# One kernel, two total orders: re-sorting the 660 operations of a convolution block and an MLP on one core

## The chip, the cores and the metric

The kernel runs on one core of a Trainium2 chip. The metric is device time in microseconds (us). Five engines with instruction queues of their own take part: TensorE (PE, matrix products and its own weight loads, PEld), VectorE (DVE), ScalarE (ACT), GpSimd (POOL) and SyncE (SP, which here does nothing but issue transfers; its queue is SPq in the profile). Each engine executes its own instructions strictly in their order and waits on semaphores for the others.

## The reference

A sequence of 2048 rows with 640 features goes through two residual blocks.

```python
x  = A_q
h  = x + A(layernorm(x), A_k, A_v, A_shift_k, A_ssm_k, A_ssm_D)
h2 = h + B(layernorm(h), w1, b1, w2)
# A: k_shift = 4-tap causal filter of k with shift_k;  kv = k_shift * v
#    y = (long causal convolution of kv with ssm_k, length 2048) + kv * ssm_D
#    returns layernorm(x) * y
# B: a = mish(layernorm(h) @ w1 + b1)          640 -> 1728
#    returns a @ w2                            1728 -> 640
```

The reference does the long convolution by FFT. The kernel does it with matrix products against tables of cosines and sines, in two factors of 128 and 16 (128 frequencies f, 16 residues), and folds `ssm_D` into the first tap of the filter.

## The kernel before

**How the work is cut.** The 640 features are five chunks of 128 (`dc` 0 to 4), the 2048 rows are 16 tiles of 128 (`t`). PSUM is used as four tiles of 128 x 1024 f32 (banks 0 to 3 below). Nearly every product stage writes one such tile, and a copy by ACT or DVE (the helper at L259 to L263: L261 is ACT, L263 is DVE) takes it back to SBUF as bf16 before the bank can be used again.

**Stages**, with the names that the order uses (a `pe` in a name is the product, an `ev` the copy that empties its bank):

- Loads by SP: `d_n` (the filter `ssm_k`, 5 x 512 KB), `d_k` and `d_v` (4 x 640 KB each), `d_g` (the table G, 8 x 512 KB), `d_x` (the rows x, 4 x 640 KB, into the place of v), `d_t2m` (a table, 1 MB), `d_w1*`, `d_w2*` (weights). ACT issues three small ones: `d_dr` (ssm_D), `d_cst` (tables), `d_sk` (the four taps). POOL issues three tiny ones for the bias b1, inside `small`.
- Filter branch: `dadd` adds D to the first tap (L370), `k1pe`/`k1ev` transpose (L376), `s1kpe`/`s1kev` (L396, L397) make 20 tiles, `s2kpe_f`/`s2kev_f` (L422) make 22 tiles of six frequencies each.
- k branch: `ktpe`/`ktev` transpose k (L341), `ktsh` shifts on POOL (L345). `cfpe` and `coef` spread the taps, and `wsh0` to `wsh3` build four filter matrices from them (L317, a tensor by tensor multiply of 1120 elements, on POOL in the order of before, with `"dve"` as a second choice in `wsh_ops`). `kspe`/`kv` filter and multiply with v (L357, L358, L362).
- Convolution: `s1vpe`/`s1vev` (20 tiles), `s2v0pe`, `s2v1pe`, `s2v2pe` with their copies (8, 4 and 8 tiles), `sw` (ten SP transfers inside SBUF that make a half-swapped copy of the filter's spectrum, L450), `pr` (20 products of spectra on DVE, L461), `i1pe`/`i1ev` (20 tiles, L479), `i2` and `y` (16 tiles, L531, L537).
- First layernorm: `ln1_t` (DVE statistics, three instructions, L510, L511), `ln1p` (three small POOL instructions, L515 to L517), `lnx` (apply; ACT L522 or POOL L524).
- Join: `wb` (L538) and `h` (L540) on DVE, `bn` (statistics, L544, L545), `pow` (two small POOL instructions, L549, L550), `hc` (apply, DVE, L559). The result is transposed: tiles 0 and 1 by PE (`trpe`, `trev`), tiles 2 to 15 by an SP transfer (`tr`, L573).
- MLP in five units of 2, 2, 4, 4, 4 tiles: `m1pe` (L598, L605) with `hb` (Mish on ACT, L620), `m2pe` (L663, L671) with `res` (DVE, L685, L688) and `d_out` (SP, L692).

**What sets the order.** One string, `ORDER`, lists every operation. `_ordered` (L108) turns it into the order in which the operations are emitted; nothing reorders them afterwards, and the waits are put in from the tiles that each operation reads and writes. A token is `name`, then `@bank` for an operation that opens a PSUM tile, or `:a`, `:d`, `:p` to put it on ACT, DVE or POOL where it has a choice.

```python
    for tok in ORDER:
        tok, _, slot = tok.partition("@")
        name, _, eng = tok.partition(":")
        o = by_name[name]
        o.eng = _LETTER[eng] if eng else o.engs[0]
        if o.psum is not None:
            o.psum.slot = int(slot)
```

So three things follow from the string and nothing else: the sequence on each engine and each transfer queue, the engine of each copy, and which PSUM bank each product uses.

Two details count below. `emit_warm` (L282) is one operation on two engines, a DVE memset and an ACT activation that waits for it. `emit_small` (L295) is two POOL memsets and three POOL transfers.

Of the kernel before, what the change touches and what calls it, by code (L numbers as in the profile page):

```python
# [25 lines left out]
ORDER = """
d_dr wz idn d_n0 cz wm@0 small lane d_n1 d_cst d_sk d_n2 warm d_n3 d_n4 d_g0 dsel dcol dadd0 d_k2 k1pe0@1 d_k3 dadd1:p k1pe1@2 d_a12 k1ev0b d_k0 k1ev0
s1kpe0_3@3 k1ev1 s1kpe0_1@0 s1kev0_3 d_k1 s1kpe0_0@1 dadd2 s1kev0_1 s1kpe1_3@2 s1kev0_0:d dadd3:p d_g4 s1kpe0_2@3 k1pe2@0 s1kev0_2 dadd4:p d_g1
s1kev1_3 kz b1pe@1 k1pe4@3 k1ev2 c_b1 cfpe@2 k1pe3@1 k1ev4:a coef d_v0 s1kpe2_0@0 k1ev3 wsh1 s1kpe2_1@2 s1kev2_0 s1kpe4_3@3 d_g7 s1kev2_1:d s1kpe3_1@1
s1kev4_3 s1kpe2_2@0 wsh3 s1kpe1_0@2 s1kev3_1 d_v1 s1kev2_2:d s1kpe4_1@3 d_g2 s1kev1_0 s1kpe3_2@1 s1kev4_1:d s1kpe1_2@0 s1kev3_2 d_g6 ktpe0_0@2 wsh2  # L30
ktpe0_3 ktpe0_2 s1kev1_2 ktpe2_0@3 ktpe2_3 ktpe2_2 d_v2 ktpe2_1 ktpe0_1 ktev2 ktpe1_0@1 ktev0:a ktpe1_1 ktpe1_3 ktpe1_2 s1kpe3_3@0 d_g5 ktev1 ktsh2
s1kpe4_0@3 s1kev3_3 s1kpe1_1@2 ktsh0 s1kev4_0:d d_v3 s1kpe4_2@1 wsh0 s1kev1_1 s1kpe3_0@0 s1kev4_2:d s1kpe2_3@3 s1kev3_0 d_g3 ktpe4_0@2 ktpe4_2 ktpe4_3
s1kev2_3 ktsh1 ktpe3_0@1 ktpe4_1 ktpe3_3 ktev4 ktpe3_1 ktpe3_2 s2kpe_6@0 s2kpe_12@3 ktev3 s2kev_6 kspe0_0@2 s2kev_12 s2kpe_18@0 kv0_0 ktsh3 kspe2_0@1
s2kev_18 ktsh4 s2kpe_42@3 kv2_0 kspe3_0@2 s2kev_42 s2kpe_96@0 kv3_0 s2kpe_24@1 s2kev_96 kspe4_0@3 s2kev_24 kspe1_0@2 kv4_0 s2kpe_108@0 kspe1_1@1 kv1_0
s2kev_108 s2kpe_72@3 kspe0_1@0 d_x1 s2kev_72 kv1_1 d_x0 s2kpe_66@2 s2kpe_102@3 s2kev_66 kv0_1 kspe4_1@1 s2kev_102 s2kpe_120@2 kv4_1 kspe3_1@0
s2kev_120 s2kpe_126@3 kv3_1 s2kpe_78@1 s2kev_126 s2kpe_0@2 s2kev_78 s2kpe_114@3 s2kev_0:d s2kpe_36@0 s2kev_114 s2kpe_54@1 s2kev_36:d s2kpe_84@2
s2kev_54 s2kpe_60@3 s2kev_84 ln1_0 kspe2_1@1 s2kev_60 s2kpe_48@0 kv2_1 ln1p0 s1vpe0_2@2 s2kev_48 s1vpe1_1@3 s1vev0_2:d s1vpe2_1@1 d_x2 s1vev1_1
s1vpe1_0@0 d_x3 s1vev2_1 s1vev1_0:d s1vpe4_3@2 s1vpe3_2@3 s1vev4_3 s1vpe0_0@1 s1vev3_2:d s1vpe2_2@0 s1vev0_0 s2kpe_90@2 s1vpe1_2@3 s1vev2_2 s2kev_90:d
s1vpe0_3@1 s1vev1_2 s1vpe1_3@0 s1vev0_3:d s1vpe0_1@2 s1vev1_3 s1vpe3_0@3 s1vev0_1:d s1vpe4_1@1 s1vev3_0 s2kpe_30@0 s1vev4_1:d s2v0pe_0@2 s2kev_30
s2v0pe_48@3 s2v0ev_0 ln1_1 sw1_0 s1vpe2_0@1 s2v0pe_64@0 sw1_1 s2v0ev_48 lnx0:p s1vev2_0:d s2v0pe_112@2 sw0_0 ln1p1 s2v0ev_64 sw4_0 s2v0pe_32@3  # L40
s2v0ev_112:d s2v0pe_80@1 sw3_1 s2v0ev_32 s1vpe3_1@0 lnx1:p sw0_1 ln1_2 s1vpe4_0@2 s2v0ev_80 sw3_0 s1vpe3_3@3 sw4_1 ln1_3 s1vev3_1 ln1p2 s1vpe2_3@1
sw2_0 s1vev4_0 s1vev3_3:d sw2_1 s1vpe4_2@0 lnx2:p s1vev4_2 s2v0pe_96@2 pr1_64 ln1p3 s2v0pe_16@3 s2v0ev_96 s2v2pe_32@0 s1vev2_3:d lnx3:p s2v0ev_16
s2v2pe_80@2 pr1_96 s2v2ev_32 s2v2pe_112@1 s2v2pe_64@3 s2v2ev_112 pr1_0 s2v2pe_48@0 s2v2ev_64 s2v2pe_0@1 pr0_96 s2v2ev_0 s2v2pe_16@3 pr1_32 s2v2ev_16
s2v1pe_96@1 pr0_64 s2v2ev_48 i1pe1_1@3 s2v2ev_80 s2v2pe_96@0 pr3_0 s2v1ev_96 i1pe1_2@2 pr3_32 i1ev1_1 s2v1pe_64@1 pr0_32 s2v2ev_96 s2v1pe_0@3 i1ev1_2
pr0_0 s2v1pe_32@0 s2v1ev_0 pr3_64 i1pe1_3@2 d_w14 s2v1ev_64 d_w10 i1pe0_2@3 pr3_96 d_w11 s2v1ev_32 d_w12 i1pe0_1@1 pr4_0 d_w13 i1ev1_3 d_t2m i1pe3_3@0
i1ev0_1 pr2_96 i1pe3_1@2 i1ev3_3 pr2_64 i1pe3_0@1 i1ev0_2 i1pe0_3@0 pr2_0 i1ev3_0 i1pe0_0@3 pr2_32 i1ev3_1 i1pe3_2@1 i1ev0_3 pr4_96 i1pe2_0@2 i1ev0_0
pr4_32 i1pe1_0@0 i1ev2_0 i1pe2_2@3 pr4_64 i1ev1_0 i1pe2_1@2 ln1_8 i1ev3_2 i1pe2_3@0 i1ev2_2 ln1_6 ln1p8 i1pe4_3@1 i1ev2_3 ln1_11 i1pe4_0@3 ln1p6
i1ev2_1 i1ev4_3:d i1pe4_2@0 i1ev4_0 lnx6:p i1pe4_1@2 ln1_4 i1ev4_2 ln1p11 i2a1@1 d_w2a i1ev4_1 ln1_14 i2a0@3 d_w2b ln1p4 d_w2c i2b1 ln1_10 i2a2@0 y1
i2b0 i2pe4@2 y0 wb1 i2pe5@1 y4 h1 i2pe8@3 wb0 y5 h0 i2b2 i2a3@2 y8 bn1 i2pe15@1 y2 i2b3 i2pe12@3 bn0 y15 pow1 i2pe13@0 y3 i2pe11@1 pow0 y12 hc1 wb2
trpe1@2 y11 i2pe7@3 hc0 y13 h2 trpe0@1 trev1:a wb3 i2pe6@0 bn2 trev0:a i2pe10@2 y7 m1pe0_3@1 h3 lnx11 pow2 bn3 m1pe0_2@3 y6 hc2 y10 pow3 ln1_7  # L50
m1pe0_1@0 tr2 lnx8 ln1p10 hc3 hb0_3 m1pe0_5@2 wb8 tr3 hb0_2 h8 ln1p7 m1pe0_6@1 ln1_9 hb0_5 m1pe0_4@3 hb0_1 ln1p14 ln1_15 m1pe0_0@2 hb0_6 lnx4 wb6 w2z
m1pe1_0@0 wb11 lnx10 wb4 lnx7:p hb0_4 m1pe1_4@1 ln1_5 ln1p15 hb1_0 m1pe1_5@3 wb7 hb0_0 h4 ln1p5 hb1_4 m1pe1_3@0 bn8 hb1_5 lnx5:p m1pe1_1@2 ln1_13
hb1_3 pow8 m1pe1_2@1 wb5 hb1_1 h6 ln1p9 lnx15 m1pe1_6@3 bn6 hb1_2 h5 i2pe9@0 pow6 hb1_6 bn4 i2pe14@2 lnx9 ln1p13 m2pe0@1 hc6 ln1_12 y9 tr6 y14 lnx13:p
bn5 lnx14 pow4 hc8 h11 pow5 tr8 m2pe1@3 wb14 h7 ln1p12 hc5 hc4 bn7 tr4 lnx12 wb10 pow7 tr5 bn11 m2pe2@0 h10 pow11 bn10 wb13 pow10 hc7 hc11 tr7 wb9
wb15 m2pe3@2 res0 tr11 h9 hc10 d_out0 h14 tr10 h15 res2 bn9 d_out2 m1pe2_3@1 wb12 pow9 bn14 h12 pow14 m1pe2_6@0 hc9 hb2_3 bn15 tr9 hc14 h13 m1pe2_5@1
tr14 hb2_6 bn12 res3 pow12 m1pe2_4@0 res1 d_out3 hb2_5 pow15 hc12 bn13 tr12 m1pe3_0@2 hc15 pow13 hb2_4 tr15 hc13 d_out1 tr13 m1pe2_0@3 hb3_0 m1pe3_2@1
hb2_0 m1pe3_6@0 hb3_2 m1pe2_1@2 hb3_6 m1pe3_5@3 hb2_1 m1pe2_2@1 hb3_5 m1pe3_1@0 hb2_2 m1pe3_3@2 hb3_1 m1pe3_4@3 hb3_3 m2pe4@1 hb3_4 m2pe6@0 m2pe5@2
res4 res6 d_out6 d_out4 m2pe7@3 m1pe4_2@1 res7 res5 d_out7 d_out5 m1pe4_5@0 m1pe4_6@3 hb4_5 hb4_2 m1pe4_4@2 hb4_6 m1pe4_3@0 hb4_4 m1pe4_0@1 hb4_3
m1pe4_1@3 hb4_0 m2pe9@2 hb4_1 m2pe11@0 m2pe8@1 res11 res9 d_out9 d_out11 m2pe10@3 m2pe15a@0 res10 res8 d_out8 m2pe12@2 res15a d_out15a d_out10
m2pe14@3 m2pe13@1 res14 res12 d_out14 d_out12 m2pe15b@0 res13 d_out13 res15b d_out15b  # L60
""".split()
# [672 lines left out]
```

## Time and profile before

| what | value |
|---|---|
| median of 3 runs | 225.41 us (225.4 to 225.89) |
| the profiled execution: span from first to last instruction | 223.5 us |
| what the median has over that span | 1.9 us |
| PE busy, ACT busy, DVE busy, POOL busy | 214.0, 133.0, 133.2, 58.9 us |
| granted TensorE clock | 1.000 throughout |

The page gives the span of the profiled execution and no second time for it. Times inside the profile count from the first instruction. "Busy" for PE includes a matmul's whole flight through the array, so two neighbours overlap and a busy PE can still be held up by its banks. A row of the timeline reads: start, duration, engine, line, operation, output from input with shapes, count; in brackets the idle time before it and what ended it. Adjacent rows of the same kind are merged, so "31.36 ... x34" is 34 copies in 31.36 us.

### The profile page before, as it was taken

The page shows a single profiled execution, that of the slowest core. Times are in us where ns is not written, and L with a number is a line of the kernel's source. Part 1 is how long each engine was busy: PE and PEld are TensorE (multiplying, and loading weights), DVE is VectorE, ACT ScalarE, POOL GpSimd, SP SyncE. Part 2 cuts the span into 40 slices and gives each one's busy share as a digit, 9 for nine tenths or more (in the row PEclk, how much of TensorE's full clock was granted, in tenths as well). Part 3 has the DMA queues.
Part 4 walks back from the last instruction along what each step waited for, and adds up shares of the span by engine and source line. Part 5 has one row for each costly group of instructions (what it writes and reads, how often), then busy time and mean ns, then how long its engine had stood idle before and what let it go on. Part 6 is the DMA issues. An engine that isn't in the chain of part 4 may idle for free.

```text
span 223.5 us, 6119 instructions
## 1 busy us (share of the span) xinstructions
PE 214.0 (96%) x2645; PEld 157.6 (70%) x2650; DVE 133.2 (60%) x232; ACT 133.0 (59%) x182; POOL 58.9 (26%) x120
## 2 busy tenths in 40 slices
...
GB/s 181 390 413 409 412 374 121 143 239 93 375 415 69 258 331 290 124 0 62 1 0 62 84 123 91 118 0 0 3 0 59 59 3 0 0 56 6 76 54 49
DMA packets 19563, 30.98 MB, mean 139 GB/s; under 512 B 10704, under 2 KB 14928, under 8 KB 18768
## 3 DMA queue, kind: packets, MB, share of 16 engines
...
q14 instruction: 6, 0.05, 0.1%
...
## 4 chain that ended last, share of the span: by engine, by line
PE 70%; DVE 13%; DMA 9%; ACT 4%; issue 2%; SPq 1%; POOL 1%; DVEq 0%
PE ps L663 26%; PE ps L598 25%; DVE ks L461 6%; DMA ks<-in_B_w_dram 4%; DMA ks<-ks 3%; PE ps L396 3%; PE ps L422 3%; ACT uv L261 3%; DMA ks<-in_A_ssm_k_dram 3%; PE ps L341 2%; PE ps L376 2%; DVE ks L263 2%; PE ps L357 2%; DVE ra L362 1%; PE ps L397 1%
## 5 line engine op out<-in xcount | busy, mean ns | idle before, releaser
L620 ACT ACTIVATE ks<-ps,b1s 128x512 bf16<-128x512 f32 (+1 forms) x69 | 36.1, 610 | 42.8 <-PE ps L598 30.3
L663 PE MATMUL ps<-ks 128*128 128x320 bf16 (+2 forms) x420 | 58.4, 299 | 0.0
L598 PE MATMUL ps<-G 128*128 128x512 bf16 (+1 forms) x320 | 57.0, 336 | 0.3
L688 DVE TENSOR_TENSOR rb<-ps,rb 128x640 bf16<-128x640 f32 x15 | 11.7, 816 | 68.9 <-PE ps L671 66.5
L663 PEld LDWEIGHTS <-ks 128*128 128x128 bf16 x420 | 40.6, 98 | 17.2 <-issue 1.3
L598 PEld LDWEIGHTS <-G 128*128 128x128 bf16 x325 | 31.3, 98 | 24.4 <-issue 1.1
L261 ACT CAST uv<-ps 128x1024 bf16<-128x1024 f32 x49 | 45.2, 1197 | 0.0
L261 ACT CAST ks<-ps 128x960 bf16<-128x960 f32 (+3 forms) x49 | 39.8, 905 | 8.1 <-PE ps L397 5.0
L461 DVE TENSOR_TENSOR ks<-ks,uv 128x2048 bf16<-128x2048 bf16 x20 | 23.1, 1225 | 0.7 <-DMA ks<-ks 0.7
L422 PEld LDWEIGHTS <-G 128*128 128x128 bf16 x512 | 20.9, 96 | 3.1 <-issue 2.5
L479 PE MATMUL ps<-a_t,ks 128*128 128x128 bf16 x320 | 18.8, 219 | 0.4 <-DVE ks L461 0.3
L479 PEld LDWEIGHTS <-ks 128*128 128x128 bf16 x320 | 18.3, 113 | 0.7 <-DVE ks L461 0.6
L422 PE MATMUL ps<-uv,G 128*128 128x64 bf16 (+1 forms) x384 | 12.8, 186 | 1.8 <-ACT uv L261 1.8
L544 DVE BATCH_NORM_STATS2 st<-rb 128x6 f32<-128x320 bf16 x32 | 14.0, 478 | 0.1
L515 POOL TENSOR_SCALAR ve<-mv 128x1 f32<-128x1 f32 x16 | 4.7, 292 | 34.9 <-DVE mv L511 34.2
L510 DVE BATCH_NORM_STATS2 st<-rb 128x6 f32<-128x320 bf16 x32 | 13.7, 471 | 0.0
L263 DVE CAST uv<-ps 128x1024 bf16<-128x1024 f32 x11 | 12.9, 1204 | 0.1
L362 DVE TENSOR_TENSOR ra<-ps,rb 128x1024 bf16<-128x1024 f32 x10 | 11.9, 1222 | 0.7 <-PE ps L358 0.5
L524 POOL TENSOR_SCALAR ra<-rb,r,nmr 128x640 bf16<-128x640 bf16 x8 | 8.9, 1118 | 10.0 <-PE ps L397 9.3
L422 PE MATMUL ps<-ks,G 128*128 128x160 bf16 x128 | 11.2, 230 | 0.0
L396 PE MATMUL ps<-cst,ra 128*64 128x128 bf16 x160 | 10.6, 219 | 0.7 <-ACT uv L261 0.5
L263 DVE CAST ks<-ps 128x1024 bf16<-128x1024 f32 (+1 forms) x9 | 10.5, 1197 | 0.5 <-PE ps L422 0.3
...
## 6 DMA issues: line engine op xcount, KB each, us to landing
ks<-ks SPq DMA_DIRECT2D x10, 512.0 KB, 6.2
G<-tab_g SPq DMA_DIRECT2D x8, 512.0 KB, 11.4
ks<-in_A_ssm_k_dram SPq DMA_DIRECT2D x5, 512.0 KB, 6.4
...
```

The costliest lines, as they stand in the source:

```text
L261: nc.scalar.copy(o, i)
L263: nc.vector.tensor_copy(o, i)
L362: nc.vector.tensor_tensor(kv_w[:, m, :, 8 * h:8 * h + 8, :], p_.f32().rearrange("p (l t d) -> p d t l", l=4, t=8), raw_v[:, 8 * h:8 * h + ...
L396: nc.tensor.matmul(ps[0:64, dgl, :], lhs, mc, start=True, stop=True)
L422: nc.tensor.matmul(p_.f32()[:, o:o + n], g_v[:, f, :], src[:, :, f, :], start=True, stop=True)
L461: nc.vector.tensor_tensor(o, o, v, ALU.mult)
L479: nc.tensor.matmul(pz[:, dgl, :], KS[:, k, b, :, l], a12[:, k, :], start=k == 0, stop=k == 1)
L510: nc.vector.bn_stats(st1[:, t, hh, :], xt(t)[:, hh * 320:(hh + 1) * 320])
L544: nc.vector.bn_stats(st2[:, t, hh, :], xt(t)[:, hh * 320:(hh + 1) * 320])
L598: nc.tensor.matmul(ph[:, o:o + w], w1[:, dc, fc * P:fc * P + P], lt[:, dc, 0:w], start=dc == 0, stop=dc == NDC - 1)
L620: nc.scalar.activation(hb[:, fc, 0:n], p_.f32()[:, i * 512:i * 512 + n], ACT.Mish, bias=b1s[:, fc:fc + 1], scale=1.0)
L663: nc.tensor.matmul(p_.f32()[:, o:o + n], lhs, w2[:, k, cols:cols + n], start=fc == 0, stop=single and fc == 13)
```

## The change

Only the string `ORDER` differs. The operations, their shapes and their number are the same. The first and the last lines of both strings, and those around the filter matrices and the first inverse products:

```diff
-d_dr wz idn d_n0 cz wm@0 small lane d_n1 d_cst d_sk d_n2 warm d_n3 d_n4 d_g0 dsel dcol dadd0 d_k2 k1pe0@1 d_k3 dadd1:p k1pe1@2 d_a12 k1ev0b d_k0 k1ev0
-s1kpe0_3@3 k1ev1 s1kpe0_1@0 s1kev0_3 d_k1 s1kpe0_0@1 dadd2 s1kev0_1 s1kpe1_3@2 s1kev0_0:d dadd3:p d_g4 s1kpe0_2@3 k1pe2@0 s1kev0_2 dadd4:p d_g1
...
-ktpe0_3 ktpe0_2 s1kev1_2 ktpe2_0@3 ktpe2_3 ktpe2_2 d_v2 ktpe2_1 ktpe0_1 ktev2 ktpe1_0@1 ktev0:a ktpe1_1 ktpe1_3 ktpe1_2 s1kpe3_3@0 d_g5 ktev1 ktsh2
...
-m2pe14@3 m2pe13@1 res14 res12 d_out14 d_out12 m2pe15b@0 res13 d_out13 res15b d_out15b
+idn d_dr wz lane d_n0 cz dsel dcol d_cst dadd0:p d_n1 wm@0 dadd1 k1pe0@1 warm d_n2 d_sk k1ev0b d_n3 d_n4 d_g0 k1pe1@2 s1kpe0_3@3 k1ev0 dadd2 k1ev1:a
+dadd3:p s1kpe0_1@0 d_k2 k1pe2@1 s1kev0_3:d d_k3 k1ev2 s1kev0_1 k1pe3@3 s1kpe0_0@2 kz dadd4:p d_a12 d_k0 s1kpe2_2@0 s1kpe2_1@1 k1ev3 cfpe@3 d_k1 coef
...
+wsh3 ktpe2_1 s1kev3_1 ktpe1_2 ktpe1_1 ktpe0_0@1 ktpe0_3 ktpe0_2 ktpe0_1 ktev1:a d_v1 s1kpe3_0@2 ktev2 s1kpe4_0@3 s1kev3_0 d_v3 s1kpe2_3@0 ktev0 ktsh2
+s1kpe1_2@1 s1kev2_3 ktsh1 s1kev4_0:d s1kpe3_2@2 s1kpe4_2@3 s1kev3_2 ktpe4_0@0 ktpe4_3 s1kev1_2 wsh1:d ktpe4_2 d_g5 ktpe4_1 ktpe3_0@2 ktpe3_2
+s1kev4_2:d ktsh0 ktpe3_1 d_g3 wsh2 s2kpe_126@3 s2kpe_120@1 ktpe3_3 ktev4 s2kev_126 small s2kev_120 s2kpe_102@0 kspe0_0@3 s2kpe_114@1 ktev3 d_g1
...
+d_out7 m2pe13@1 m2pe15b@3 d_out10 res14 d_out11 res12 res13 d_out12 d_out8 d_out14 res15b d_out9 d_out15a d_out13 d_out15b
```

Engine by engine, the differences that are spoken of below:

- **ACT's head.** Before: `d_dr d_cst d_sk warm s1kev0_3`. Now: `d_dr d_cst warm d_sk k1ev1`. On DVE the memset of `warm` now stands behind `dadd1`, which waits for the second filter load.
- **POOL.** Before: `idn small dadd1 dadd3 dadd4 kz wsh1 wsh3 wsh2 ktsh2 ktsh0 wsh0 ktsh1 ktsh3 ktsh4`. Now: `idn dadd0 dadd3 kz dadd4 wsh0 wsh3 ktsh2 ktsh1 ktsh0 wsh2 small ktsh4 ktsh3`.
- **DVE around the k transposes.** Before: `ktev2 ktev1 s1kev4_0 s1kev4_2 ktev4 ktev3`. Now: `ktev2 ktev0 s1kev4_0 wsh1 s1kev4_2 ktev4 ktev3`; `ktev1` is ACT's.
- **Copies per engine**, filter branch up to `s2k`: 16 on ACT in both (14 casts `s1kev`, one `k1ev`, one `ktev`). `s2kev`: ACT 19 and DVE 3 before, 18 and 4 now. `s1vev`, `s2v*ev`, `i1ev` together: ACT 49 and DVE 11 before, 48 and 12 now. `y0`, `y9`, `y14` and `trev0` go from ACT to DVE; the copy of the bias, `c_b1`, goes from 12.65 us behind the spectra of v.
- **SP.** The loads of v and G are interleaved differently behind `d_k1` (now `g6 g7 v2 g4 v0 v1 v3 g5 g3 g1 g2`); only `d_x0` is ahead of the ten `sw`; `d_x2` and `d_t2m` stand behind the sixth `sw`, `d_x1` and `d_x3` among the loads of w1, `d_w2c` behind `tr3`. The transposing transfers of unit 2 go out as `tr6 tr4 tr7 tr5` (before: `tr6 tr8 tr4 tr5 tr7`).
- **DVE statistics of the first layernorm.** Before the first `wb`, ten tiles are done in the order of before (0 1 2 3 8 6 11 4 14 10) and five now (2 1 0 3 4).
- **MLP.** The tiles of the hidden layer come in another order, and some `m1pe` stand between `m2pe`s; all `m1pe0`, `m1pe1`, then `m2pe0` to `m2pe3` still come first, and `m2pe13`, `m2pe15b` last.

59 lines of the change are left out of this document (29 added, 30 removed).

## The prediction

> **What bounds the kernel now.** I read the table of windows first (columns: stretch, then busy us and instruction count of PE, PEld, DVE, ACT, POOL, the granted clock, the DMA share, GB/s).
>
> ```profile
> 27.45:91.20 63.75, 60.07 (x1318) 56.66 (x1316) 61.68 (x75) 61.47 (x68) 16.04 (x30) 1.00 0.68 251
> 99.50:130.60 31.10, 31.10 (x263) 23.93 (x260) 27.96 (x77) 19.50 (x40) 21.84 (x47) 1.00 0.24 46
> 130.60:220.50 89.90, 89.64 (x558) 51.17 (x561) 18.74 (x38) 25.70 (x42) 4.31 (x10) 1.00 0.14 38
> ```
>
> From 99.5 on PE is never free: transposed tiles, MLP, end. From the first `s2k` product (27.45) to the last `i1` copy (91.2) ACT is busy 61.47 of 63.75 us and DVE 61.68: emptying PSUM is the limit. Next I read the timelines and the chain of waits for the seams.
>
> ```profile
> 27.45 1.00 PE L422 MATMUL ps<-ks,G 128*128 128x160 bf16 x12
> 36.97 8.38 ACT L261 CAST ks<-ps 128x960 bf16<-128x960 f32 x10 [0.25 <-PE ps L422]
> 59.80 31.36 ACT L261 CAST uv<-ps 128x1024 bf16<-128x1024 f32 x34
> 72.87 16.70 PE L479 MATMUL ps<-a_t,ks 128*128 128x128 bf16 x288
> 91.20 1.03 PE L531 MATMUL ps<-uv,ra 128*128 128x128 bf16 x7 [0.77 <-ACT uv L261]
> 99.49 1.25 PE L598 MATMUL ps<-G 128*128 128x256 bf16 x10
> ...
> 83.35 8.18 DMA ks<-in_B_w_dram
> 91.53 0.69 ACT ks L261
> ```
>
> A copy costs ACT 0.84 us (8.38/10) in `s2k` and 0.92 (31.36/34) afterwards. PE's `i1` products run without a gap from 72.87 too, 18 tiles in 16.70, so 0.92 each: there PE, ACT and DVE are level, and an order can win only by starting the stage earlier or taking copies off ACT. The seam is 91.20 (`i2` lacks only the last `i1` copy) to 99.49 (first `m1`). So the time is the start of `m1` plus a fixed 121 us of PE work, unless a tile comes late. The last two rows are the chain's, which has ACT's first `y` (91.53) wait for the w2 load; that load writes another place than y, and `i2b1` ends just there, so I take the last `i1` copy for the cause. The sum is made on the span, 223.5; the 1.9 us that the median has over it I leave as they are.
>
> **The change part by part.**
>
> *Stage 1, to the first `s2k` product.* Same 16 copies on ACT.
>
> ```profile
> 7.20 1.20 PE L376 MATMUL ps<-ident,ks 128*128 128x128 bf16 x16 [0.42 <-DMA ks<-in_A_ssm_k_dram]
> 9.01 3.76 ACT L261 CAST ks<-ps 128x1024 bf16<-128x1024 f32 x4 [5.00 <-PE ps L397]
> 12.65 0.19 ACT L499 CAST b1s<-ps 128x14 f32<-128x14 bf16 x1
> 15.30 5.59 ACT L261 CAST ks<-ps 128x1024 bf16<-128x1024 f32 x6
> 21.43 1.86 ACT L261 COPY uv<-ps 128x2048 bf16<-128x2048 bf16 x1 [0.54 <-PE ps L341]
> 21.19 2.49 DVE L263 COPY uv<-ps 128x2048 bf16<-128x2048 bf16 x2 [1.56 <-PE ps L341]
> 23.60 2.35 DVE L263 CAST ks<-ps 128x1024 bf16<-128x1024 f32 x2
> 24.10 0.32 SPq L325 DMA_DIRECT2D G<-tab_g  x1
> G<-tab_g SPq DMA_DIRECT2D x8, 512.0 KB, 11.4
> sk_r<-in_A_shift_k_dram ACTq DMA_DIRECT2D x1, 5.0 KB, 4.9
> a_t<-tab_t2m SPq DMA_DIRECT2D x1, 64.0 KB, 9.8
> ```
>
> ACT now begins with `k1ev1` right behind `k1pe1`, at 8.44 (7.20 + 1.20) instead of 9.01. I walked both queues and the four banks by hand with these rows (ACT cast 0.93, ACT transposed copy 1.86, DVE cast 1.17, a bank free when its copy ends): `k1pe2` at 9.3, `cfpe` at 13.0, the k transposes from 18.95, the last casts at 26.6 (ACT) and 26.9 (DVE), first `s2k` at 26.95. Term: 0.5 earlier. In it are `dadd1` ahead of `k1ev0b` on DVE (0.6 later, covered by `k1pe1`) and `wsh1` on DVE. No row shows the latter: at the rate of the dense bf16 multiply (1.225 us for 2048, row L461 below) it is 0.67, at that of the f32 casts (1.22 for 1024) 1.33. I take 1.25, since one factor repeats each value 32 times and is not dense.
>
> *`wsh1` beside `wsh2`.* Both multiply two SBUF tensors, and the new order starts them almost together.
>
> ```profile
> 19.28 3.07 PE ps L341 x24
> 22.48 0.61 POOL L345 COPY uv<-uv 128x508 bf16<-128x508 bf16 x1 [1.69 <-DVE uv L263]
> 23.92 2.07 POOL L317 TENSOR_TENSOR rw<-cst,coef 128x1120 bf16<-128x1120 bf16 x1
> 59.25 0.87 POOL L524 TENSOR_SCALAR ra<-rb,r,nmr 128x640 bf16<-128x640 bf16 x1
> 60.20 1.07 POOL L515 TENSOR_SCALAR ve<-mv 128x1 f32<-128x1 f32 x1
> 62.39 2.87 POOL L524 TENSOR_SCALAR ra<-rb,r,nmr 128x640 bf16<-128x640 bf16 x1
> 59.82 1.37 DVE L461 TENSOR_TENSOR ks<-ks,uv 128x2048 bf16<-128x2048 bf16 x1
> 62.24 2.35 DVE L461 TENSOR_TENSOR ks<-ks,uv 128x2048 bf16<-128x2048 bf16 x2
> L461 DVE TENSOR_TENSOR ks<-ks,uv 128x2048 bf16<-128x2048 bf16 x20 | 23.1, 1225 | 0.7 <-DMA ks<-ks 0.7
> ```
>
> In these rows POOL's 128x1 addition takes 1.07 and ends when the DVE multiply of 59.82 does; the apply of 0.87 takes 2.87 under two such multiplies. The other way round, the multiply of 59.82 takes 1.37 (others 1.22) while POOL's apply still runs to 60.12. So whichever is first seems to keep the other out until it ends. Who is first: let `ktev0` end on DVE at e. `ktev1` on ACT got its data eight transposes earlier (8 of 3.07/24, 1.0 us) and takes 1.86 against 1.24 (2.49/2), so it ends at e-0.4; POOL then does `ktsh1` (to e+0.27) and `ktsh0` (0.61), and starts `wsh2` at e+0.84. DVE does `s1kev4_0` (1.14 further) and comes to `wsh1` at e+1.06. POOL is first by 0.2 us, and `wsh1` waits 2.07-0.2, some 1.75. Behind it on DVE stands `s1kev4_2`, for which every `s2k` product waits. Bounds: 0 (DVE first; `wsh2` has 10 us of slack) and 1.75. I take 1.75. The Trainium skill, "SBUF — State Buffer", section "Who interferes with whom", says the same: a DVE instruction with two SBUF inputs and a GpSimd instruction that reads SBUF exclude each other for a whole instruction, and issue order decides. By that rule the term is 1.75; by DVE's mean rows alone it would be 0.
>
> *Spectra, 27.45 to 91.2.* ACT loses one `s2k` and one later copy (0.84 + 0.92) and gains `c_b1` (0.19): 61.47 - 1.6 = 59.9. Walking the banks I find 2.8 us idle against 2.3 (two copies stand ahead of others whose products come first), so 62.7 against 63.75. Term: 1.05 earlier. DVE takes two copies (2.3) and sheds five statistics before the end (1.04 each: 85.63 - 84.59, rows below). The `sw` go out when the last `s2k` copy is done; `d_x2` and `d_t2m` (1.7 MB) now precede the last four, which by the walk leaves `pr3` 0.7 of cover; without that, DVE stands as long as the transfer is late. The loads of v and G keep their volume, so the last lands near 35.5 again (24.10 + 11.4); it is now `d_g2`, which the walk reads at 38.1 (later still if `wsh1` waits), and `d_g1` ahead of it has 1.0 us. `small` moves on POOL to ahead of `ktsh4` and `ktsh3`, whose readers come 5 us later; its three transfers are read at 64 us. `c_b1` and `b1pe` sit in gaps at 64.
>
> *Seam.* `y0` on DVE beside `y1` on ACT, and `trev0` on DVE while ACT does `y8`: by the walk 8.0 us from the last `i1` copy to `m1` against 8.29. Term: 0.3 earlier.
>
> *MLP.* PE work is the same. The debt is DVE's: five more statistics, `y9` and `y14`, fewer tiles of `bn`, `h`, `wb` before `hc7`.
>
> ```profile
> 99.49:126.60 27.11, 23.97 (x69) 1.00 0.21 38
> 126.20 0.80 DVE L559 TENSOR_SCALAR rw<-rb,mv,r 128x640 bf16<-128x640 bf16 x2
> 126.67 1.20 SPq L573 DMA_TRANSPOSE G<-rw  x1
> G<-rw SPq DMA_TRANSPOSE x14, 2.6
> 130.62 0.82 PE L598 MATMUL ps<-G 128*128 128x512 bf16 x2
> 84.59 0.88 DVE L510 BATCH_NORM_STATS2 st<-rb 128x6 f32<-128x320 bf16 x2
> 85.63 0.83 DVE L510 BATCH_NORM_STATS2 st<-rb 128x6 f32<-128x320 bf16 x2
> L538 DVE TENSOR_TENSOR ks<-ks,ra 128x640 bf16<-128x640 bf16 x4 | 1.9, 485 | 0.5 <-ACT ks L261 0.5
> L688 DVE TENSOR_TENSOR rb<-ps,rb 128x640 bf16<-128x640 f32 x15 | 11.7, 816 | 68.9 <-PE ps L671 66.5
> ```
>
> DVE did 23.97 us of work from `m1`'s start to `hc7`. Now +5 `ln1` (5.2), +2 `y` (1.5, less than twice the 0.82 of L688, since neighbours overlap), -2 `bn` (2.1, the same three instructions as `ln1`), -3 `h`, -3 `wb`, -1 `hc` (2.7, at 0.49 less the overlap): 25.9. Then `tr7` and behind it `tr5` (1.3 + 2.6): 29.8 after `m1`'s start, while PE needs it at 31.1 (130.62 - 99.49). Slack 1.3 less DVE's idle, which was 3.1 before and which I walk to 0.6 (`hc5` waits for `pow5`; the other small POOL steps have a statistic between them and their reader). Term: 0. The load `d_w2c` and `d_x3` are 8 us early. At the end `m2pe13`, `m2pe15b` and their transfers stand as before.
>
> Sum: -0.5 + 1.75 - 1.05 - 0.3 = -0.1. On 225.41 that is 225.3.
>
> **The rivals.**
>
> *No exclusion, or DVE first.* Without the 1.75: 225.41 - 1.85 = 223.6. For it: POOL's lead is only 0.2 us on a walk that is good to 0.3, and one row (1.37) carries the DVE side.
>
> *The statistics come due.* If DVE idles 3.1 us before `hc7` as it did, `tr5` lands 31.1 + 1.8 after `m1`'s start, PE stands 1.8 at the first `m1pe2`, and the time is 227.1. It decides from 1.3 us of idle on. For it: the idle of before was waits for POOL and ACT, and POOL's small steps stretch under DVE's two-input operations. Against it: `pow4`, `pow6`, `pow7` are ready ahead by the walk.
>
> *The taps come late.* `d_sk` now waits for the second filter load (7.2) through `warm`, goes out at 7.7 and lands at 12.6 if it takes its 4.9 again; `cfpe` is due at 13.0. With the 9.8 of the 64 KB load of that time it lands at 17.5: PE stands 4.5 us, and the time is 229.8.
>
> **How the numbers follow.** Forecast 0.44, no exclusion 0.28, statistics due 0.20, taps late 0.08. The walk is good to about 0.8 us, so the forecast's own range is 224.5 to 226.1. Within 0.3% (0.7 us, about what three runs can tell from no change) is 224.7 to 226.1: the forecast lies there with 0.25 of its 0.44, faster with 0.09, slower with 0.10. The first rival is faster (0.27 of 0.28). The second is slower with 0.15 and level with 0.05, the third slower. Faster 0.36, level 0.31, slower 0.33. The range 223.2 to 227.2 leaves out the lower third of the first rival and the third.
>
> **What would show it.** In the changed kernel: a DVE row of L317 near 24.5 that lasts near 3 us beside a POOL row of L317 of 2.07 (right), or 1.3 (first rival); the first L422 product at 28.6 or 27.0; the last `i1` copy 62.7 us later; L598 8.0 us after that; no PE gap before the first 512-wide L598. Wrong would be a PE gap ahead of L304, or copies that wait for banks more than I walked: each unseen 0.1 us on one of some 60 copies in a row adds up here.

## The result and the profile after

The changed kernel takes 227.48 us in the median (four runs, 227.07 to 229.13) beside 225.41 (225.02 to 225.89) for the kernel before on the same chip: a ratio of 1.0104, 95% interval 1.0068 to 1.0141. It is slower by 2.1 us. The prediction was 225.3, with a range up to 227.2.

The profiled execution took 227.25, with a span of 225.5 (before 223.5). Its table of windows has the stretches of before, each from the same event to the same event (columns: stretch, then busy us and instruction count of PE, PEld, DVE, ACT, POOL, the granted clock, the DMA share, GB/s).

```profile
28.43:91.47 63.04, 59.62 (x1319) 56.77 (x1320) 59.95 (x62) 60.34 (x67) 8.19 (x18) 1.00 0.65 235
99.83:131.84 32.01, 31.31 (x260) 23.85 (x260) 30.43 (x83) 17.50 (x35) 21.86 (x47) 1.00 0.22 40
131.84:222.20 90.36, 89.93 (x563) 51.24 (x561) 23.70 (x50) 24.86 (x42) 9.68 (x20) 1.00 0.14 37
```

Set beside the rows of before, the difference of 1.9 us lies here:

| stretch | before | after | difference | the prediction's term |
|---|---|---|---|---|
| start to the first L422 | 27.45 | 28.43 | +0.98 | +1.25 (-0.5 and +1.75) |
| spectra, to the last `i1` copy | 63.75 | 63.04 | -0.7 | -1.05 |
| seam, to the first L598 | 8.29 | 8.36 | +0.1 | -0.3 |
| first two MLP units, to the first 512-wide L598 | 31.10 | 32.01 | +0.9 | 0 |
| from there to the end of the span | 92.9 | 93.6 | +0.7 | 0 |

So the start went as predicted, and 1.6 us came from the two places that were put at nothing. The timelines and the chain of waits of the changed kernel show the three places. First the rows of DVE, POOL, PE and SP (start, duration, engine, line, what; in brackets the idle time before and what ended it):

```profile
24.16 3.00 DVE L317 TENSOR_TENSOR rw<-cst,coef 128x1120 bf16<-128x1120 bf16 x1
27.08 1.21 DVE L263 CAST ks<-ps 128x1024 bf16<-128x1024 f32 x1
23.90 2.07 POOL L317 TENSOR_TENSOR rw<-cst,coef 128x1120 bf16<-128x1120 bf16 x1
28.43 0.37 PE L422 MATMUL ps<-ks,G 128*128 128x160 bf16 x3 [1.63 <-DVE ks L263]
107.79 7.27 PE L598 MATMUL ps<-G 128*128 128x256 bf16 x65 [0.70 <-DMA G<-rw]
102.68 1.31 SPq L573 DMA_TRANSPOSE G<-rw  x1
104.09 2.55 SPq L573 DMA_TRANSPOSE G<-rw  x1
219.38 1.92 SPq L692 DMA_DIRECT2D out_dram<-rb  x1
222.86 0.39 SPq L692 DMA_DIRECT2D out_dram<-rb  x1
221.80 0.42 DVE L685 TENSOR_TENSOR rb<-ps,rb 128x256 bf16<-128x256 f32 x1 [0.70 <-PE ps L663]
```

`wsh1` on DVE lasts 3.00 us and ends 1.2 after `wsh2` on POOL; behind it `s1kev4_2` (27.08), and for that the first L422 waits. At 107.79 the second MLP unit starts late: it waits for `tr3`, whose issue took SP 2.55 us (1.22 before). At the end the last sum is done at 222.22, but its output is issued at 222.86, since SP's queue is behind, with one issue of 1.92 us in it. Before, that output was issued 0.02 us after its sum. The chain of the changed kernel (start, length, what):

```profile
103.69 0.31 DVE rw L559
104.00 0.09 DVE st L510
104.09 3.66 DMA G<-rw
107.75 0.05 issue
```

`tr3` lands 3.66 us after its issue; the median of all transposes before was 2.6. The table of transfers for 104 to 107 us and for 218.5 to 221.5 (queue, kind: packets, MB, share of the 16 transfer engines) shows a second kind of traffic in both places, one packet of 16 KB each:

```profile
q8 instruction: 1, 0.02, 2.8%
...
q8 instruction: 1, 0.02, 3.4%
```

In the trace these packets lie at 104.84 (1.36 us long) and 219.31 (1.62). There are 21 of them, and between the later ones TensorE executes about 256 instructions (from 179.68 to 201.68 us 132 matmuls and 131 weight loads, from 201.68 to 219.31 130 and 129), so I take them for TensorE's program; experiment 2 tests that. Before, the one near `tr3` came at 105.42, after the last of `tr3`'s own packets (105.30).

### The profile page after: what moved, and what is told of

Same layout as the page of the kernel before. It is cut to its first block, busy times and chain, and to the rows that moved or that the text cites. A ratio compares the mean times of both kernels' runs of the same rounds, so it can differ in the third digit from the quotient of the medians.

```text
span 225.5 us, 6131 instructions
## 1 busy us (share of the span) xinstructions
PE 213.9 (95%) x2650; PEld 157.5 (70%) x2650; DVE 141.7 (63%) x239; ACT 128.5 (57%) x174; POOL 56.8 (25%) x121
## 4 chain that ended last, share of the span: by engine, by line
PE 77%; DVE 12%; DMA 4%; ACT 3%; issue 2%; SPq 0%; DVEq 0%; ACTq 0%
PE ps L663 26%; PE ps L598 22%; PE ps L479 8%; PE ps L422 7%; PE ps L396 3%; ACT uv L261 3%; DVE ks L263 2%; DMA ks<-in_A_ssm_k_dram 2%; DVE uv L263 2%; PE ps L376 2%; DMA G<-rw 2%; DVE ra L362 2%; PE ps L357 2%; PE ps L341 2%; DVE st L544 1%
## 5 line engine op out<-in xcount | busy, mean ns | idle before, releaser
L598 PE MATMUL ps<-G 128*128 128x512 bf16 (+1 forms) x325 | 57.8, 337 | 0.8 <-DMA G<-rw 0.7
L598 PEld LDWEIGHTS <-G 128*128 128x128 bf16 x325 | 31.3, 98 | 25.2 <-issue 1.3
L261 ACT CAST ks<-ps 128x960 bf16<-128x960 f32 (+3 forms) x45 | 37.3, 897 | 5.2 <-PE ps L422 2.7
L422 PEld LDWEIGHTS <-G 128*128 128x128 bf16 x512 | 20.8, 96 | 4.8 <-issue 4.2
L479 PE MATMUL ps<-a_t,ks 128*128 128x128 bf16 x320 | 19.1, 219 | 0.6 <-issue 0.6
L479 PEld LDWEIGHTS <-ks 128*128 128x128 bf16 x320 | 18.3, 113 | 0.8 <-issue 0.8
L515 POOL TENSOR_SCALAR ve<-mv 128x1 f32<-128x1 f32 x16 | 4.0, 251 | 51.2 <-DVE mv L511 50.6
L263 DVE CAST uv<-ps 128x1024 bf16<-128x1024 f32 x12 | 14.2, 1208 | 0.7 <-PE ps L397 0.6
L422 PE MATMUL ps<-uv,G 128*128 128x64 bf16 (+1 forms) x384 | 12.7, 187 | 1.8 <-ACT uv L261 1.2
L263 DVE CAST ks<-ps 128x1024 bf16<-128x1024 f32 (+2 forms) x13 | 14.1, 1101 | 0.4 <-PE ps L397 0.2
L422 PE MATMUL ps<-ks,G 128*128 128x160 bf16 x128 | 11.2, 230 | 1.8 <-DVE ks L263 1.6
L549 POOL TENSOR_SCALAR ve<-mv 128x1 f32<-128x1 f32 x16 | 4.7, 294 | 26.7 <-DVE mv L545 26.3
```

What stands on the lines that cost most here:

```text
L261: nc.scalar.copy(o, i)
L263: nc.vector.tensor_copy(o, i)
L422: nc.tensor.matmul(p_.f32()[:, o:o + n], g_v[:, f, :], src[:, :, f, :], start=True, stop=True)
L479: nc.tensor.matmul(pz[:, dgl, :], KS[:, k, b, :, l], a12[:, k, :], start=k == 0, stop=k == 1)
L598: nc.tensor.matmul(ph[:, o:o + w], w1[:, dc, fc * P:fc * P + P], lt[:, dc, 0:w], start=dc == 0, stop=dc == NDC - 1)
```

## The experiments

All were timed beside the kernel before, on the same chip. The ratio is to it; the changed kernel itself stands at 1.0104, and at 1.0089 in a second timing.

| kernel | median us | ratio, 95% interval | span us |
|---|---|---|---|
| `a1_apart`: `wsh2` away from `wsh1` | 225.87 | 1.0011 (0.9992 to 1.0030) | 223.5 |
| `b1_outs`: last outputs in order | 227.02 | 1.0074 (1.0050 to 1.0099) | 224.6 |
| `c1_fetch`: instruction packets moved, at the start | 228.18 | 1.0109 (1.0078 to 1.0141) | 225.9 |
| `d1_seam`: `w2z` later | 227.26 | 1.0074 (1.0048 to 1.0100) | 225.9 |
| `e2_cover`: PE work ahead of the second unit | 227.00 | 1.0067 (1.0050 to 1.0084) | 224.9 |
| `e1_all`: a1, b1, d1, e2 together | 224.50 | 0.9953 (0.9937 to 0.9970) | 221.9 |
| `f1_bcoll`: before, with the collision | 228.90 | 1.0144 (1.0121 to 1.0167) | 227.1 |
| `f2_bfetch`: before, instruction packets moved | 225.53 | 1.0003 (0.9987 to 1.0019) | 223.3 |
| `g1_fetch`: instruction packets moved, in a pause | 226.81 | 1.0072 (1.0040 to 1.0104) | 225.0 |
| `a0_after`: the changed kernel again | 227.69 | 1.0089 (1.0060 to 1.0119) | 226.4 |
| `h1_loads`: two loads later | 226.48 | 1.0040 (1.0013 to 1.0068) | 224.4 |
| `h2_all`: e1 and h1 together | 223.19 | 0.9889 (0.9850 to 0.9928) | 223.2 |

Differences between two of these kernels of less than about 0.7 us aren't separated by the times; there the rows decide.

**1. Is it exclusion, or what the multiply costs on DVE?** `a1_apart`, the changed kernel with

```diff
-wsh3 ktpe2_1 ... ktpe3_1 d_g3 wsh2 s2kpe_126@3
+wsh3 wsh2 ktpe2_1 ... ktpe3_1 d_g3 s2kpe_126@3
```

> The changed kernel with one move: `wsh2` (GpSimd) stands right after `wsh3`, in GpSimd's idle stretch at 18.07, and no longer beside `wsh1` on VectorE. Theory (the two engines shut each other out): `wsh1` on VectorE falls from 2.99 us to about 1.25, `s1kev4_2` ends near 26.5, the first L422 starts near 26.7 instead of 28.43, and the time falls by 1.5 to 1.75, to about 225.8. Rival (the multiplication costs VectorE 3 us by itself): `wsh1` stays at 3.0 and the time at 227.5. Second rival (the start of the spectra matters little, because the loads or the copies there end no earlier): L317 is short, but the last copy before the second multiplications stays near 91.5 and the time within 0.3 of 227.5.

```profile
24.02 1.31 DVE L317 TENSOR_TENSOR rw<-cst,coef 128x1120 bf16<-128x1120 bf16 x1
25.25 1.22 DVE L263 CAST ks<-ps 128x1024 bf16<-128x1024 f32 x1
13.89 6.11 POOL L317 TENSOR_TENSOR rw<-cst,coef 128x1120 bf16<-128x1120 bf16 x3 [2.63 <-DVE coef L309]
26.62 0.73 PE L422 MATMUL ps<-ks,G 128*128 128x160 bf16 x8
```

These are timeline rows of `a1_apart`. The same multiply at the same place on DVE takes 1.31 us, the first L422 starts at 26.62 instead of 28.43, and the time falls by 1.6. The theory holds; both rivals fall. With this one token moved, the changed order is level with the kernel before.

The other way round, `f1_bcoll` puts the collision into the kernel before:

```diff
-d_v0 s1kpe2_0@0 k1ev3 wsh1 s1kpe2_1@2 ... s1kev4_2:d
+d_v0 s1kpe2_0@0 k1ev3 s1kpe2_1@2 ... wsh1:d s1kev4_2:d
```

> The kernel before with one edit: `wsh1` goes to VectorE between `s1kev4_0` and `s1kev4_2` (24.8 us), while GpSimd's `wsh0` runs (23.92 to 25.99). Theory (mutual exclusion): `wsh1` lasts 2.2 to 2.4 us although VectorE alone needs about 1.3, `s1kev4_2` ends near 28.3 instead of 25.95, the first L422 starts near 28.45 instead of 27.45, and the time rises by 0.8 to 1.1, to about 226.3. Rival (without exclusion): `wsh1` takes 1.3, `s1kev4_2` ends at 27.3, the first L422 stays within 0.1 of 27.45 and the time at 225.4.

```profile
24.53 2.44 DVE L317 TENSOR_TENSOR rw<-cst,coef 128x1120 bf16<-128x1120 bf16 x1
26.90 1.21 DVE L263 CAST ks<-ps 128x1024 bf16<-128x1024 f32 x1
23.72 2.07 POOL L317 TENSOR_TENSOR rw<-cst,coef 128x1120 bf16<-128x1120 bf16 x1
25.73 1.71 POOL L345 COPY uv<-uv 128x508 bf16<-128x508 bf16 x1
28.17 1.63 PE L341 MATMUL ps<-ident,ra 128*128 128x128 f32 x10 [1.95 <-DVE ks L263]
29.59 0.74 PE L422 MATMUL ps<-ks,G 128*128 128x160 bf16 x4
```

`wsh1` lasts 2.44 us beside POOL's multiply, as expected; and POOL's next copy, 0.61 us elsewhere, lasts 1.71 and ends 0.47 after `wsh1` does. So the lock goes from POOL to DVE and back. The first L422 came at 29.59, not at 28.45, and the time at 228.90, not at 226.3: I had overlooked that ten k transposes (L341) need the bank that `s1kev4_2` empties, and so stand between it and L422. That makes 2.1 of the 3.6 us. The rest goes with the clock: in that execution the table of windows gives a granted clock of 0.85 from 29.59 to 40.00. The one run of the five with a mean clock of 0.998 took 227.59, 2.3 over the kernel before; the four at 0.991 or 0.992 took 228.83 to 229.08. None of the 17 runs beside them was under 0.998, so the edit may bring the lower clock on; why is open.

**2. What holds `tr3` and the last output up?** My theory was the 16 KB instruction packet. It can be moved without touching a transfer: more instructions on TensorE ahead of it bring it earlier. `c1_fetch` put 48 more matmuls into the warming at the start:

```diff
-WARM = 9
+WARM = 57
...
-        for _ in range(WARM):
-            nc.tensor.matmul(wm_p.f32()[:, 0:512], wz[:, 0:P], wz[:, P:D], start=True, stop=True)
+        for i in range(WARM):
+            if i < 5:
+                nc.tensor.matmul(wm_p.f32()[:, 0:512], wz[:, 0:P], wz[:, P:D], start=True, stop=True)
+            else:
+                nc.tensor.matmul(wm_p.f32()[0:32, 0:32], wz[:, 0:32], wz[:, P:P + 32], start=True, stop=True)
```

> The changed kernel with 48 more tiny matmuls (32x32) in the warming at the start and 4 of the 512-wide ones left out, so that the 16 KB instruction transfer that fell at 104.84 us, on the transposes, comes about 96 TensorE instructions, some 5 us, earlier. Theory (that transfer held the transposes up): L573's second issue takes 1.2 to 1.3 us instead of 2.55, its landing comes 2.6 to 2.7 us after its issue instead of 3.66, the matmuls of the second MLP unit wait at most 0.1 us instead of 0.88, and the time falls by 0.7 to 1.0. If the tail's 1.92 us issue goes too, which had such a transfer beside it, the last output gains up to 0.6 more. Rival (the transposes are held up by something else, for instance the weight loads): L573's second issue stays at 2.5 and the wait at 0.9; the time stays within 0.3 of 227.5, or rises by what the longer warming costs the first stage.

The pause is gone, the late output too: from the first L598 to the end of the span it took 124.06 us, where the changed kernel took 125.64 and the kernel before 124.06. But the time did not fall: beside the 1.6 that the MLP gained, the first stage lost 1.1 and the spectra 1.3 (experiment 5 shows the same spectra without this edit). The chain of the first stage has a wait for the taps, the transfer of my third rival. The product that spreads them started at 13.12 instead of 12.67, which is 0.4 of the 1.1 (first L422 at 29.51); the rest of it was not traced:

```profile
7.44 5.64 DMA sk_r<-in_A_shift_k_dram
```

So the verdict on the time had to come from a kernel that leaves the first stage alone. `g1_fetch` has the 48 tiny matmuls in the pause of 1.6 us that TensorE has anyway ahead of L422, and `a0_after` is the changed kernel again, beside it:

```diff
 # in ktpe3_1, behind its two transposes
+                if (m, a) == (3, 1):
+                    for _ in range(48):
+                        nc.tensor.matmul(o[0:32, 0, 3, 0:32], ident[:, 0:32], ident[:, 0:32], start=True, stop=True)
```

> The changed kernel with 48 tiny matmuls (32x32, some 30 ns each) put into TensorE's pause of 1.9 us ahead of the first L422 instead of into the warming at the start, so that only the places of the 16 KB instruction transfers behind it move, by about 96 TensorE instructions, and the first stage stays as it is. Theory (those transfers cost the changed kernel 0.9 at `tr3` and 0.6 at the last output): the first L422 stays at 28.4, no pause ahead of the second MLP unit, the last output issued within 0.1 us of `res15b`, from the first L598 to the end 124.1 instead of 125.6, and the time falls by 1.3 to 1.6, to about 226.0. Rival (the better end of the kernel with the longer warming came from something else in that run): the pause and the late output are back, time 227.5.

> The changed kernel itself, timed beside the run above on the same chip, as the measure for it. Every theory expects 227.1 to 227.6, a pause of 0.9 to 1.0 us ahead of the second MLP unit, and the last output issued 0.5 to 0.7 us after `res15b`; should the pause be missing, the transfer's place would vary from one execution to the next and not hang on TensorE's count of instructions.

Timeline rows of `a0_after`, PE:

```profile
100.91 7.26 PE L598 MATMUL ps<-G 128*128 128x256 bf16 x65
108.82 7.27 PE L598 MATMUL ps<-G 128*128 128x256 bf16 x65 [0.65 <-DMA G<-rw]
```

and of `g1_fetch` (line numbers 3 higher), PE, SP and DVE:

```profile
100.91 14.35 PE L601 MATMUL ps<-G 128*128 128x256 bf16 x130
219.58 0.45 SPq L695 DMA_DIRECT2D out_dram<-rb  x1
222.46 0.33 SPq L695 DMA_DIRECT2D out_dram<-rb  x1
222.00 0.42 DVE L688 TENSOR_TENSOR rb<-ps,rb 128x256 bf16<-128x256 f32 x1 [0.70 <-PE ps L666]
```

Both start the MLP at 100.91. In `a0_after` the two units are 65 and 65 products with a pause between them, in `g1_fetch` 130 in one piece. The packet that lay 5.06 us after the first L598 in `a0_after` (105.97) lies 0.43 after it here (101.34), before the transposes. SP's issue near the end is 0.45 instead of 1.87 us, the last output goes out 0.04 after its sum, and from the first L598 to the end it takes 124.07 instead of 125.5. The times, 226.81 and 227.69, go the same way by 0.9, where 1.3 to 1.6 was expected, with intervals that overlap; three of the twelve runs of `g1_fetch` had a clock of 0.992 and took 228.7 to 229.2. So it is the rows that show it, and all fourteen traces agree with them. In the nine where such a packet begins 0.6 to 1.2 us after the issue of `tr3`, `tr3` lands 3.3 to 3.7 us after its issue; in the five where none does it lands after 2.6. The long issue is not needed for it: in five of the nine the issue of `tr3` took its usual 1.22, and the landing was late all the same. So both late terms of the changed kernel have one cause: where TensorE's instruction packets fall.

In the kernel before the same can be done the wrong way round. `f2_bfetch` has 18 tiny matmuls in place of the ninth warming one.

> The kernel before with 18 tiny matmuls in place of the last of the nine warming ones, so that the 16 KB instruction transfer that came at 105.42, after `tr3` had landed, comes about 34 TensorE instructions or 1.9 us earlier, near 103.5, onto `tr3` (issued at 103.16). Theory (that transfer holds the transposes up): `tr3` lands 3.5 to 4 us after its issue instead of 2.6, the second MLP unit waits 0.2 to 0.8 us where it waited for nothing, and from the first L598 to the end it takes 124.3 to 124.9 instead of 124.06. Rival: `tr3` lands 2.6 after its issue and no pause appears; what the time gains or loses comes from before the first L598.

The packet came at 102.08, earlier than aimed, and met `tr2`: its issue took 1.99 us instead of 1.31, so `tr3` was issued 4.35 us after the first L598 instead of 3.67. It landed 6.95 after it, and the second unit is due at about 7.0. No pause, 124.06 to the end, no change in time. So what the rival had announced came out: `tr3` landed 2.6 after its issue, since the packet had missed it and met `tr2`. What is seen is a delay of 0.7 by the packet, at no cost: the kernel before has 0.7 us of cover there (the transposes land that much ahead of their need), and this took it up to the last 0.05.

**3. Can the cost be covered instead?** `e2_cover` gives TensorE other work until `tr3` is there:

```diff
-m1pe1_4@0 h7 ln1_8 ... m1pe1_6@3 h6 hb1_1 pow4 wb5 i2pe9@1 ln1p11 hb1_6 y9:d ... i2pe14@0 ... y14:d
+i2pe9@0 i2pe14@2 y9:d y14:d m1pe1_4@3 h7 ln1_8 ... m1pe1_6@0 h6 hb1_1 pow4 wb5 ln1p11 hb1_6 ...
```

The products between the two places take the banks that lie two steps on in the rotation 0, 2, 3, 1.

> The changed kernel with `i2pe9` and `i2pe14` moved from behind the second MLP unit to ahead of it, and their evictions `y9`, `y14` with them. Theory (TensorE lost 0.88 us there because it had nothing else to do until `tr3` landed): no TensorE pause before the second unit, the time from the first L598 to the end shrinks from 125.6 to about 124.7, the time to about 226.6. Rival (VectorE's chain to the third unit is next in line, so the pause comes back ahead of `m1pe2`): a pause of 0.5 to 1 us near 130, time unmoved.

```profile
107.17 1.25 PE L531 MATMUL ps<-uv,ra 128*128 128x512 bf16 x8
108.25 2.35 PE L598 MATMUL ps<-G 128*128 128x256 bf16 x20
110.79 5.07 PE L598 MATMUL ps<-G 128*128 128x256 bf16 x45 [0.19 <-DVE ks L263]
```

In these PE rows of `e2_cover` no wait for a transfer is left, though `tr3` landed as late as ever (3.6 us after its issue). A wait of 0.19 for a bank, which DVE's `y9` empties, is new. From the first L598 to the end: 124.86, expected 124.7.

`b1_outs` gets SP's queue out of the way at the end, without moving the instruction packet:

```diff
-res8 hb4_2 ... res9 ... res11 res15a d_out7 ... d_out11 res12 res13 d_out12 d_out8 d_out14 res15b d_out9 d_out15a d_out13 d_out15b
+res8 d_out8 hb4_2 ... res9 d_out9 ... res11 d_out11 res15a d_out15a d_out7 ... res14 d_out14 res12 res13 d_out12 res15b d_out13 d_out15b
```

> The changed kernel with its last outputs issued in the order in which their sums get done (`d_out8`, `d_out9`, `d_out11`, `d_out15a`, `d_out14` right behind `res8`, `res9`, `res11`, `res15a`, `res14`), so that `d_out12`, `d_out13`, `d_out15b` alone stand behind `res12`. Theory (SP's queue held the last output back): the last issue comes within 0.1 us of the end of `res15b` instead of 0.63 after it, the time falls by 0.5 to 0.7, to about 226.9. Rival (the last transfer's own flight and not the queue sets the end): the time stays within 0.2 of 227.5.

```profile
222.05 0.33 SPq L692 DMA_DIRECT2D out_dram<-rb  x1
221.60 0.42 DVE L685 TENSOR_TENSOR rb<-ps,rb 128x256 bf16<-128x256 f32 x1 [0.70 <-PE ps L663]
```

The last output is issued 0.03 after its sum (timeline rows of `b1_outs`), although the packet is there as before, at 219.30. So the tail needed two things together: seven outputs queued behind `res12`, and a packet on one of them. Either taken away is enough.

**4. The seam.** `d1_seam` moves `w2z` on POOL:

```diff
-i2pe11@3 w2z lnx3:p i2pe4@1 ... lnx6:p lnx7 wb7
+i2pe11@3 lnx3:p i2pe4@1 ... lnx6:p w2z lnx7 wb7
```

> The changed kernel with `w2z`, two fills on GpSimd of 1.30 us, moved from ahead of `lnx3` to behind `lnx6`. `lnx3` then starts at about 91.3 instead of 92.61 and is over before `wb1` on VectorE begins. Theory (the seam's chain on VectorE pays for the exclusion of `wb1` by `lnx3`): `wb1` takes 0.45 us instead of 1.07, the first L598 starts 0.5 to 0.6 us earlier after the last copy of the stage before it, and the time falls by 0.5 to 0.6. Rival (the seam waits for GpSimd's rsqrt or TensorE instead): first L598 unmoved, time within 0.2 of 227.5.

The DVE row of the changed kernel, two `wb` from 92.75 on, beside `lnx3` on POOL (92.61 to 93.48):

```profile
92.75 1.47 DVE L538 TENSOR_TENSOR ks<-ks,ra 128x640 bf16<-128x640 bf16 x2
```

and of `d1_seam`, where `lnx3` is over at 93.44:

```profile
93.98 0.88 DVE L538 TENSOR_TENSOR ks<-ks,ra 128x640 bf16<-128x640 bf16 x2
```

From the first L531 to the first L598 it takes 9.10 us instead of 9.57. That is the seam's missing gain, again DVE and POOL excluding each other. But the changed kernel does not pay it in every execution: in `a0_after`, with `w2z` in its old place, `wb` came later beside `lnx3` (at 94.30, `lnx3` from 93.56 to 94.43), lasted 0.89, and this stretch took 9.10 too. The time of `d1_seam`, 227.26, shows little of the gain: in that execution the first load landed 0.7 us later than in the changed kernel's, and the first L422 came at 29.14.

**5. The spectra.** From the start of the first L422 to that of the last L479, `a0_after` and `g1_fetch` took 63.2 and 63.1 us, the changed kernel's first profile 61.8. The difference is pauses of TensorE in the middle of a tile, put down to "issue", that is to nothing that the profile shows. PE rows of `a0_after`, and its counts from the start (table of windows, PE and PEld with their counts):

```profile
66.51 0.25 PE L422 MATMUL ps<-uv,G 128*128 128x32 bf16 x4 [0.98 <-issue]
72.47 0.55 PE L479 MATMUL ps<-a_t,ks 128*128 128x128 bf16 x7 [0.96 <-issue]
...
0.00:66.50 66.50, 59.00 (x1246) 53.34 (x1247) 55.06 (x61) 54.46 (x58) 17.07 (x37) 1.00 0.71 266
0.00:72.45 72.45, 64.00 (x1372) 58.19 (x1373) 60.59 (x66) 60.06 (x65) 17.07 (x37) 1.00 0.73 276
```

and of `g1_fetch`, which has 48 matmuls more ahead of them:

```profile
63.36 0.75 PE L425 MATMUL ps<-uv,G 128*128 128x64 bf16 x20 [0.26 <-issue]
70.58 0.53 PE L482 MATMUL ps<-a_t,ks 128*128 128x128 bf16 x6 [1.78 <-issue]
...
0.00:63.35 63.35, 60.15 (x1246) 53.88 (x1247) 51.96 (x59) 51.58 (x56) 17.08 (x37) 1.00 0.70 268
0.00:70.57 70.57, 65.03 (x1373) 58.36 (x1373) 58.60 (x64) 58.17 (x63) 17.08 (x37) 1.00 0.73 276
```

The pauses stand behind the same matmul numbers, 1246 and 1372 or 1373, whatever those matmuls are: other tiles, 2 to 3 us earlier. They are 126 matmuls and as many weight loads apart, which is what a wait for TensorE's own next packet of instructions looks like. The packets themselves show the rest: eight of the traces have the second pause, and in each TensorE goes on 1.25 to 1.41 us after a packet has ended (in `a0_after` at 72.47 after 71.22, in `g1_fetch` at 70.58 after 69.27). The Trainium skill, "Advanced Engine Details and Errata", section "ISA Cache", gives a cache line of 16 KB or 256 instructions; packets and pauses of these traces agree (16 KB, 252 to 263 instructions). The kernel before has no such pause. In it the packets come earlier by TensorE's own count: the one ahead of the second pause began when 2678 matmuls and weight loads had started in the changed kernel (2694 in `a0_after`), 2571 in the kernel before. What differs is how long the transfer engines stay full; their share stands in the second-last column of the table of windows. Changed kernel:

```profile
64.00:68.00 4.00, 3.28 (x92) 3.13 (x92) 4.00 (x5) 4.00 (x6) 0.00 (x0) 1.00 0.96 309
68.00:72.00 4.00, 3.35 (x80) 3.19 (x77) 4.00 (x4) 3.91 (x6) 0.00 (x0) 1.00 0.92 383
```

and the kernel before:

```profile
64.00:68.00 4.00, 2.86 (x81) 2.47 (x78) 3.31 (x4) 4.00 (x5) 1.25 (x1) 1.00 0.96 389
68.00:72.00 4.00, 4.00 (x113) 3.91 (x111) 4.00 (x4) 4.00 (x6) 0.00 (x0) 1.00 0.07 25
```

So a full share alone makes no pause: until 68 the engines are as full in the kernel before.

`h1_loads` takes the two loads away that the new order put there:

```diff
-sw2_0 s2v0pe_0@0 d_x2 pr1_96 ... s1vev2_3 d_t2m pr0_32 ... i1pe1_0@2 d_w13 s2v1ev_64
+sw2_0 s2v0pe_0@0 pr1_96 ... s1vev2_3 pr0_32 ... i1pe1_0@2 d_w13 d_x2 d_t2m s2v1ev_64
```

> The changed kernel with two loads, `d_x2` (128 x 5120 bytes) and `d_t2m` (128 x 8192), moved from among the shuffles of the spectra (issued at 57.95 and 59.57) to behind `d_w13` (72.75). Theory (the 16 transfer engines are 96 to 100% busy from 56 to 72 us, TensorE's own instruction transfers stand in that queue, and TensorE pauses for 0.5 to 2.0 us in the middle of a tile, waiting for nothing that the profile shows): the share of the transfer engines falls below 0.5 in 68 to 72, the pauses put down to issue in 62 to 76 vanish, the stretch from the first L422 to the last L479 comes to 61.0 to 61.8 instead of 61.8 to 63.2, and the time falls by 0.4 to 1.5, to about 226.8. Rival (the pauses are matmul records that are missing from the trace): the pauses vanish or not, and the stretch stays at 61.8 or more, the time at 227.5.

```profile
64.00:68.00 4.00, 3.20 (x91) 2.95 (x88) 4.00 (x5) 4.00 (x5) 0.00 (x0) 1.00 0.55 225
68.00:72.00 4.00, 4.00 (x107) 3.90 (x103) 4.00 (x4) 4.00 (x7) 0.00 (x0) 1.00 0.01 4
```

No pause put down to issue is left in 62 to 76, TensorE is busy throughout 68 to 72, and the stretch takes 60.9 us, 1.0 less than the 61.9 of the kernel before. The time falls by 1.0 to 1.2. The rival (records missing from the trace) falls. So the two loads are the cause, but the pauses are only one of two ways in which they cost. The other is a row of DVE in the changed kernel:

```profile
72.66 1.23 DVE L461 TENSOR_TENSOR ks<-ks,uv 128x2048 bf16<-128x2048 bf16 x1 [0.29 <-DMA ks<-ks]
```

This is `pr3_0`, which waits for a shuffle (`sw`). The last four shuffles stand in the queue behind the two loads and land 9.7 to 11.3 us after their issue; in `h1_loads` they land after 6.6 to 6.7, and no `pr` waits. In `a1_apart`, `e2_cover` and `e1_all` the pauses between 62 and 76 come to only 0.20 to 0.25 us, but there `pr3_0` waits 0.56 to 0.78, and the stretch takes 61.6 to 61.8 as in the changed kernel's first profile. So in those executions the late shuffle sets the length; only in the ones with pauses of 1.9 us and more (`a0_after`, `g1_fetch`) do the pauses lengthen it further.

**6. All together.** `e1_all` is a1, b1, d1 and e2 in one order, `h2_all` adds h1.

> The changed kernel with four repairs together: `wsh2` behind `wsh3`, the last outputs in the order of their sums, `w2z` behind `lnx6`, and `i2pe9`, `i2pe14` (1.19 us of TensorE) between the first and the second MLP unit as cover for the second transposes. Theory (the four costs lie one behind the other on the path): 1.6 from the apart multiplications, 0.5 to 0.9 from the tail, 0.5 from the seam, 0.9 from the cover, less what was already gone with another: a time of 223.3 to 224.2, below both kernels. Rival (each repair uncovers the next limit, so that they don't add up): 225 or more.

> The four repairs together (`wsh2` behind `wsh3`, the last outputs in the order of their sums, `w2z` behind `lnx6`, `i2pe9` and `i2pe14` ahead of the second MLP unit) and `d_x2` and `d_t2m` behind `d_w13` as well. The four alone took 224.50. Theory (the loads starve TensorE's instructions): 0.2 to 0.8 less, about 224.0, and less spread from run to run. Rival (with the other repairs the shuffles come at another time and nothing is starved): 224.5.

`e1_all` took 224.50, a little over the range expected but below both kernels: 0.9953 (0.9937 to 0.9970). Of the 3.6 us by which its span is shorter than the changed kernel's, 1.7 are the first L422 (26.76), 0.5 the seam, 1.3 the MLP and the end. `h2_all` took 223.19: 0.9889 (0.9850 to 0.9928) of the kernel before, so some 2.3 us faster than it and 4.3 than the changed kernel. Its profiled execution is no measure for the last step, since its clock fell to 0.94 between 60 and 91 us. The step from `e1_all` to `h2_all` is 1.3, where 0.2 to 0.8 was expected; `e1_all`'s trace shows a wait of 0.56 before `pr3_0` and a pause of 0.20, and the rest was not traced. Less spread was expected too and did not come: the runs go from 222.97 to 225.03, the two longest with a clock of 0.992 and 0.991.

## Why the prediction was wrong

- **Exclusion, +1.75: right.** `wsh1` lasted 3.00, POOL was first by 0.26 (walked: 0.2), and taking POOL away gave back 1.8 at the first L422 (28.43 to 26.62). (The sum's wait was a slip: 2.07 - 0.2 is 1.87, not 1.75; measured is 3.00 - 1.31, so 1.69.) The rule of the Trainium skill that was weighed there ("SBUF — State Buffer", "Who interferes with whom") decided the sign rightly. The 1.25 for the multiply alone measured 1.31. The first rival (no exclusion) fell.
- **Stage 1, -0.5: right in sign, under-sized.** Without the collision the first L422 comes at 26.62, 0.8 earlier than before; predicted was 26.95.
- **Spectra, -1.05: under-reached, -0.7; the step "Walking the banks I find 2.8 us idle" was right, the sentence on the loads was not.** ACT's idle time in the stretch is 2.70 (63.04 - 60.34), close to the walk; its busy time fell by 1.1 instead of 1.6, and what kept it up was not traced. I had written that `d_x2` and `d_t2m` "now precede the last four", which "leaves `pr3` 0.7 of cover". In the changed kernel `pr3_0` waited 0.29 for its shuffle, in three repaired ones 0.56 to 0.78, so that cover was not there. And the same loads held up TensorE's instructions, which the walk left out: pauses of 0.8 us between 62 and 76 in the profiled execution, 1.9 in the next one. With the two loads out of the way the stretch is 1.0 shorter than in the kernel before (`h1_loads`).
- **Seam, -0.3: wrong, +0.1.** The walk had the exclusion rule at hand and did not apply it to `wb1` beside `lnx3`; undone, the seam gives 0.5.
- **MLP, 0: the failing step, "Then `tr7` and behind it `tr5`".** The walk for `tr5` held (it landed at 129.70 and was needed at 131.84), so the second rival fell too. But the debt to the second unit was never walked: `tr3` goes out 4.26 after the first L598 instead of 3.67, its cover falls from 0.7 to about 0.1, and the instruction packet then costs 0.9. That it needed both is shown from two sides: in `f2_bfetch` 0.7 of cover swallows a packet's delay of 0.7, and in `g1_fetch` `tr3` goes out as late (4.25 after the first L598) and costs nothing without the packet.
- **The end, "`m2pe13`, `m2pe15b` and their transfers stand as before": wrong, +0.6 on SP's queue.** The diff itself showed seven outputs gathered behind `res12`; I looked at PE and not at SP.
- **The taps** were not late in the changed kernel (`cfpe` at 12.66), so the third rival fell there.

The sum by steps that were looked at would have been about +0.4 (0.98 - 0.7 + 0.1); the miss is the 1.6 of steps that were put at zero because TensorE's work there was the same.
